# Retention and two feed-forward layers on one core: six weight slices converted beside the retention instead of nine, in halves, and PE filled while unit 1 loads

## The chip, the core and the metric

The kernel runs on one core of one Trainium2 chip. The metric is the device time of one execution in microseconds. Engines are named as in the profile: PE multiplies matrices (PEld is its weight load), DVE, ACT and POOL work element by element, and SP issues transfers; ACT and POOL issue some too.

## What is computed

Cut to what matters:

```python
# q, k, v: (4 batches, 8 heads, 768 positions, 64), float32
state = gamma[h] * state + outer(k[t], v[t])      # per batch and head, over t
y[t]  = q[t] @ state / 8
x = y as (3072 tokens, 512)
x = gelu_sigmoid(x @ w_in)  @ w_out               # 512 -> 2048 -> 512, first layer
x = relu(x @ w2_in) ** 2    @ w2_out              # 512 -> 2048 -> 512, second layer
```

## The kernel before, in words

**Retention.** The 3072 positions are cut into 24 units of 128 positions (six to a batch, all eight heads together). A unit is a block of 128 x 2048 floats (1.05 MB), loaded by SP in two halves of 0.52 MB: first q and k transposed for the scores, then k and v by position. There are five unit buffers, so SP issues unit u + 4 when the outputs of unit u - 1 have been computed. Iteration u of the loop at L564 puts in the queues: the scores of unit u on PE (L456) and its scaled values `vs` (on POOL for u < 6 and every third unit, L475, else eight small products on ACT, L480); for u = 2 to 5 the split of a unit of the first token block into a high and a low part (`split_0`, ACT L491 and DVE L492); the outputs of unit u - 1 on PE (L508, L519, L530); and then, within `cv_step`, the mask of unit u on DVE (L465) and the scaling of the outputs of unit u - 1 (L543, L547, L550). The scores have one buffer in PSUM: the scores of unit u + 1 wait for the mask of unit u.

**Weights of the first layer.** They come as 64-bit floats in 32 slices of 0.52 MB (16 steps f, each with one slice for up and one for down) and are converted on the chip: a load by POOL (`cv_load`, L119), two scalings on ACT (`cv_a`, L124 and L125), three operations on DVE (`join` in two steps, L129 and L134, `round_up`, L142), then a high part on ACT (`cv_high`, L157) and a low part on DVE (`cv_low`, L162). `cv_step` does one slice; in the retention it is given the mask and the scaling, which it queues between its own DVE operations. In the units of `CVU` a slice is converted, nine in all. `cv_step` there starts with `cv_a`, and loads begin at unit 2. The other 23 slices are converted in token block 0 of the first layer, seven in every four f.

**First layer.** Four blocks of 512 tokens (n = 0 to 3). For every f, `up(n, f)` gives PE 12 matmuls of 512 columns (L595 to L597), then ACT makes g and its high part gh (L602, L603) and DVE the low part gl (L607). `down(n, f - 2)` follows on PE with 12 more (L626 to L628); every third of them reads gl. After `up(3, 15)` come `down` of f = 13, 14 and 15 in a row, and then the second layer.

**Background.** The weights of a faster scheme for the rest of the work are made beside the layer by the generator `maker`. `background(us)` (L378) adds a credit and takes steps from `maker` until the credit is used up; each step states its own price in its `yield`. ACT's part of a step is put in `acts` and is queued only at the next call of `background`. Where `maker` needs such a part, it yields None, the call ends and the credit left over is capped at 3.0. `make_first` has 16 jobs, `make_second` 32 (lines 301 to 356). One call is made after every f but the last, as soon as the conversions are done. Each call gives `BG` = 4.8, but `BG - 1.6` = 3.2 for f >= 5 of block 3. In these f a step of `x_operands` (DVE, 128 x 1024) is queued as well: it prepares the next blocks, whose data `x_loads` fetches with POOL at f = 3.

Of the kernel before, what the change touches and what calls it, by code (L numbers as in the profile page):

```python
# [10 lines left out]
F32 = mybir.dt.float32  # L11
F32R = mybir.dt.float32r
BF16 = mybir.dt.bfloat16
U32 = mybir.dt.uint32
U16 = mybir.dt.uint16
ACTF = mybir.ActivationFunctionType
ALU = mybir.AluOpType
PSUM = bass.MemoryType.PSUM

P = 128  # L20
B, H, S, D = 4, 8, 768, 64
NT, DM, DFF = 3072, 512, 2048
NP = H // 2
CPB = S // P
NU = B * CPB
KD = DM // P
# [4 lines left out]
WA = 8  # L31
LOOK = 2
WARM = 10
UNITS = 5
# [6 lines left out]
NSTD = 4  # L41
SLOTS = 8
EARLY = 2
BG = 4.8
CVU = (5, 8, 11, 14, 17, 20, 21, 22, 23)
RAWS = 5
BGUP = 1.8

# [9 lines left out]
def tile_retention_then_two_ffns(  # L58
# [10 lines left out]
    nc = tc.nc  # L69
# [16 lines left out]
    cv_p = cv_ctx.enter_context(tc.tile_pool(name="cv", bufs=2, side="right"))  # L86
# [10 lines left out]
    order = []  # L97
# [5 lines left out]
            order.append((f, 1))  # L103
    wpool = {f: wa_p for f in range(WA)}
    ws = {}
    cv = {"load": 0, "a": 0, "b": 0, "pool": None, "ahead": 3}
    cvt = {}

    def cv_load():
        n = cv["load"]  # L110
        if n == len(order):
            return
        if n >= cv["b"] + cv["ahead"]:
            return
        cv["load"] += 1
        f, s = order[n]
        raw = cv_p.tile([P, 512, 2], U32, tag="raw", name=f"raw{n}", bufs=RAWS)
        src = w1[f, :, s * 512:(s + 1) * 512].bitcast(U32)
        nc.gpsimd.dma_start(out=raw, in_=src.rearrange("p (c t) -> p c t", t=2))  # L119
        cvt[n] = raw  # L120

    def scale_words(hm, raw):

        nc.scalar.mul(hm, raw[:, :, 1].bitcast(F32), 2.0 ** -112)  # L124
        nc.scalar.mul(raw[:, :, 0], raw[:, :, 0], 2.0 ** -29)  # L125

    def join(out, hb):

        v.tensor_scalar(  # L129
            out=out, in0=hb, scalar1=3, scalar2=0x7FFFFFFF,  # L130
            op0=ALU.logical_shift_left, op1=ALU.bitwise_and,
        )
        yield
        v.scalar_tensor_tensor(  # L134
            out=out, in0=hb, scalar=0x80000000, in1=out, op0=ALU.bitwise_and, op1=ALU.bitwise_or
        )
        yield

    def round_up(w, raw):

        half = w.bitcast(U16).rearrange("p (c t) -> p c t", t=2)[:, :, 0]
        v.scalar_tensor_tensor(out=half, in0=half, scalar=65527.0, in1=raw[:, :, 0], op0=ALU.min, op1=ALU.add)  # L142

    def cv_a():

        n = cv["a"]
        if n == min(cv["load"], cv["b"] + 2):
            return
        cv["a"] += 1
        scale_words(cvt[n][:, :, 1].bitcast(F32), cvt[n])  # L150

    held = deque()

    def cv_high():
        if held:
            w, hm, key = held[0]
            nc.scalar.copy(out=w[:, :, 0], in_=hm.rearrange("p (k c) -> p k c", c=P))  # L157

    def cv_low():
        if held:  # L160
            w, hm, key = held.popleft()
            v.tensor_tensor(  # L162
                out=w[:, :, 1], in0=hm.rearrange("p (k c) -> p k c", c=P), in1=w[:, :, 0], op=ALU.subtract
            )
            ws[key] = w

    def cv_step(limit=len(order), f1=None, f2=None, load=True):

        n, ready = cv["b"], cv["a"]
        if cv["pool"] is not None and limit is not None:  # L170
            cv_a()
        cv_high()
        if limit is None or n >= min(limit, ready):
            for f in (f1, f2):
                if f is not None:
                    f()
            cv_low()
        else:
            cv["b"] += 1
            raw = cvt.pop(n)  # L180
            key = order[n]
            hm = cv_p.tile([P, 512], F32, tag="hm", name=f"hm{n}")
            w = wpool[key[0]].tile([P, 4, 2, P], F32R, tag=f"w{key[1]}", name=f"w{n}")
            steps = join(hm.bitcast(U32), raw[:, :, 1])
            next(steps)
            if f1 is not None:
                f1()
            next(steps)
            round_up(hm, raw)
            if f2 is not None:  # L190
                f2()
            cv_low()
            held.append((w, hm, key))
        if limit is None:
            return
        if cv["pool"] is None:
            cv_a()
        if load:
            cv_load()
            cv_load()  # L200

    def weights(f, s):
        while (f, s) not in ws:
            if held:
                cv_high()
                cv_low()
            else:
                cv_step()
        return ws[f, s][:, :, 0], ws[f, s][:, :, 1]
# [168 lines left out]
    def background(us):  # L378

        credit[0] += us  # L380
        while acts:
            acts.popleft()()
        while credit[0] > 0:
            c = next(maker, None)
            if c is None:
                credit[0] = min(credit[0], 3.0)
                return
            credit[0] -= c
# [5 lines left out]
    hl = {}  # L394
# [15 lines left out]
    with tc.manual_schedule():  # L410

        with (
# [10 lines left out]
            warm_sb = att.tile([P, 512], BF16, tag="warm", name="warm_sb", bufs=1)  # L423
# [17 lines left out]
            def load_unit(u, parts=(0, 1024, 2048)):  # L441
                if u >= NU:
                    return
                if u not in units:
                    units[u] = att.tile([P, 2048], F32, tag="unit", name=f"unit{u}", bufs=UNITS)
                for a, z in zip(parts, parts[1:]):
                    nc.sync.dma_start(out=units[u][:, a:z], in_=qkv[u, :, a:z])
# [36 lines left out]
            def split_0():  # L484

                xt, cols = pend.pop("x", (None, None))
                if xt is None:
                    return
                for k in range(KD):
                    hi, lo = hl[0][k]  # L490
                    nc.scalar.copy(out=hi[:, cols], in_=xt[:, k, :])  # L491
                    nc.vector.tensor_tensor(  # L492
                        out=lo[:, cols], in0=xt[:, k, :], in1=hi[:, cols], op=ALU.subtract
                    )

            def banked(t):
                return t.rearrange("p (k b) i -> p b k i", b=2)
# [54 lines left out]

                return scaled

            load_unit(0, (0, 512, 1024))
            nc.sync.dma_start(out=tab_sb, in_=tab)
            load_unit(1, (0, 1024))
            load_unit(0, (1024, 2048))
            load_unit(1, (1024, 2048))
            nc.sync.dma_start(out=ytab_sb[0], in_=ytab)  # L560
            for u in range(2, UNITS):
                load_unit(u)

            for u in range(NU + 1):  # L564
                masked = scores(u) if u < NU else None
                split_0()
                scaled = outputs(u - 1) if u > 0 else None
                if 0 < u < CPB:
                    for p in range(NP):
                        nc.scalar.mul(ytab_sb[u][:, p, :], ytab_sb[0][:, p, :], ystep_sb[:, u, p:p + 1])  # L570
                if u == 18:
                    cv["ahead"] = RAWS
                cv_step(2 * WA if u in CVU else 0, masked, scaled, u >= 2)
                if u > 0:
                    load_unit(u + UNITS - 1)

# [13 lines left out]
        def up(n, f):  # L590
            hi, lo = weights(f, 0)
            hp = hp_p.tile([P, TB], F32, tag="h", name=f"h{n}_{f}")
            for k in range(KD):
                xh, xl = hl[n][k]
                nc.tensor.matmul(hp, lo[:, k], xh, start=(k == 0), stop=False)  # L595
                nc.tensor.matmul(hp, hi[:, k], xh, start=False, stop=False)  # L596
                nc.tensor.matmul(hp, hi[:, k], xl, start=False, stop=(k == KD - 1))  # L597
            g = g_p.tile([P, TB], F32, tag="gs", name=f"gs{n}_{f}", bufs=1)
            gh = g_p.tile([P, TB], F32R, tag="gh", name=f"gh{n}_{f}")
            gl = g_p.tile([P, TB], F32R, tag="gl", name=f"gl{n}_{f}")  # L600

            nc.scalar.activation(out=g, in_=hp, func=ACTF.Gelu_apprx_sigmoid)  # L602
            nc.scalar.copy(out=gh, in_=g)  # L603
            gs[n, f] = (gh, gl)

            def low():
                v.tensor_tensor(out=gl, in0=g, in1=gh, op=ALU.subtract)  # L607

            if n == 0 and cv["b"] < len(order):
                cv_step(len(order), None, low)  # L610
                if f % 4 < 3:
                    cv_step()
            else:
                low()
                if f < NF - 1:

                    background(BG if n < NSTD - 1 or f < 5 else BG - 1.6)

        def down(n, f):
            hi, lo = weights(f, 1)  # L620
# [233 lines left out]
        ready = deque()  # L854
# [212 lines left out]
```

## Time and profile before

| | us |
|---|---|
| median of 3 runs (1058.65 to 1060.0) | 1058.9 |
| profiled execution | 1059.31 |
| its span | 1057.5 |
| PE busy within the span | 1040.0 |
| DVE busy | 746.1 |
| ACT busy | 523.5 |

The span is the time from the first to the last instruction in the profile; 1.8 us lie around it. All times of rows are microseconds from the start of the span. "Busy" of PE counts matmuls whose ends are modelled, so it says where PE has work, not how fast it runs; the speed is seen from the distance between the starts of equal groups and from the granted clock.

### The profile page before, as it was taken

The numbers are of one execution on the slowest core, as the hardware profiler recorded it, in microseconds if no ns is written. First come the engines' busy times: TensorE is split into PE (matmuls) and PEld (weight loads), VectorE is DVE, ScalarE is ACT, GpSimd is POOL, SyncE is SP. The second block draws the span as 40 slices with busy tenths as digits, with TensorE's granted clock in tenths as the row PEclk, the third lists the DMA queues.
The fourth block names the chain that finished last, engine by engine and source line by source line (L and its number), as shares of the span: only waits on it lengthen the run. The fifth ranks groups of instructions, "written<-read, shape, count | busy, mean of one in ns | idle before, by whom it ended". The sixth has DMA issues, their size and how long they took to land.

```text
span 1057.5 us, 15484 instructions
## 1 busy us (share of the span) xinstructions
PE 1040.0 (98%) x5642; PEld 859.7 (81%) x5642; DVE 746.1 (71%) x1069; ACT 523.5 (49%) x858; POOL 101.5 (10%) x147
## 2 busy tenths in 40 slices
PE   7999999999999999999999999999999999999998
PEld 5887888888888888887888888888888888888886
DVE  3889997986787869753599344888345886455953
ACT  3768774434655667554546233455233464233443
POOL 2212210111111121110000100000100000000000
PEclk9999999999999999999999999999999999999999
DMA  9996879645588687799666876667876667766664
GB/s 342 366 405 219 329 257 357 248 189 191 201 262 268 236 306 255 261 349 321 191 214 217 269 236 193 192 208 225 302 197 192 188 216 232 218 193 188 209 205 161
DMA packets 106651, 259.34 MB, mean 245 GB/s; under 512 B 11216, under 2 KB 11344, under 8 KB 106320
## 3 DMA queue, kind: packets, MB, share of 16 engines
q1 hardware_dynamic: 79088, 156.64, 46.4%
q0 software_dynamic: 22304, 83.89, 22.5%
q10 hardware_dynamic: 5184, 17.83, 4.7%
q8 instruction: 45, 0.74, 0.3%
q14 instruction: 30, 0.25, 0.1%
HBM read 184.91 MB, written 73.40 MB: 244 GB/s over the span
## 4 chain that ended last, share of the span: by engine, by line
PE 92%; DMA 5%; DVE 1%; ACT 1%; SPq 0%; issue 0%; POOL 0%; ACTq 0%; POOLq 0%; DVEq 0%
PE D L769 29%; PE X L769 16%; PE Z L769 8%; PE h L595 6%; PE y L628 6%; PE y L626 5%; PE y L627 5%; PE h L596 5%; PE h L597 5%; PE Y L769 4%; DMA r<-kw 2%; DMA unit<-qkv 2%; PE yp L508 1%; PE sc L456 1%; DMA raw<-w 1%; DVE pt L465 1%
## 5 line engine op out<-in xcount | busy, mean ns | idle before, releaser
L769 PE MATMUL D<-gx,r 128*128 128x512 f32 x1344 | 306.4, 389 | 0.0
L769 PEld LDWEIGHTS D<-gx,r 128*128 128x128 f32 x1344 | 252.1, 188 | 53.0 <-DVE gx L872 0.8
L871 ACT CAST gx<-g 128x1024 fp32r<-128x1024 f32 x112 | 116.6, 1051 | 93.1 <-PE D L769 83.5
L872 DVE TENSOR_TENSOR gx<-g,gx 128x1024 fp32r<-128x1024 f32 x112 | 136.3, 1219 | 36.9 <-ACT gx L871 36.7
L769 PE MATMUL X<-xh,r 128*128 128x512 f32 x512 | 157.9, 390 | 1.1 <-DMA r<-kw 1.0
L790 ACT COPY g<-X 128x512 f32<-128x512 f32 x96 | 56.5, 589 | 188.9 <-PE X L769 188.9
L795 DVE TENSOR_TENSOR g<-Z,g 128x512 f32<-128x512 f32 x64 | 44.2, 691 | 147.5 <-ACT g L790 101.4
L769 PEld LDWEIGHTS X<-xh,r 128*128 128x128 f32 x512 | 95.8, 188 | 22.3 <-issue 2.7
L595 PE MATMUL h<-hl,w 128*128 128x512 f32 x256 | 99.7, 389 | 0.0
L628 PE MATMUL y<-gl,w 128*128 128x512 f32 x256 | 99.7, 389 | 0.0
L769 PE MATMUL X<-xl,r 128*128 128x512 f32 x256 | 99.6, 389 | 0.0
L627 PE MATMUL y<-gh,w 128*128 128x512 f32 x256 | 99.6, 389 | 0.0
L597 PE MATMUL h<-hl,w 128*128 128x512 f32 x256 | 99.6, 389 | 0.0
L626 PE MATMUL y<-gh,w 128*128 128x512 f32 x256 | 99.6, 389 | 0.0
L596 PE MATMUL h<-hl,w 128*128 128x512 f32 x256 | 99.6, 389 | 0.0
L769 PE MATMUL Z<-xh,r 128*128 128x512 f32 x256 | 79.0, 390 | 0.7 <-DMA r<-kw 0.7
L603 ACT CAST gh<-gs 128x512 fp32r<-128x512 f32 x64 | 39.8, 622 | 72.3 <-PE y L627 71.6
L607 DVE TENSOR_TENSOR gl<-gs,gh 128x512 fp32r<-128x512 f32 x64 | 44.1, 689 | 36.6 <-ACT gh L603 36.4
L602 ACT ACTIVATE gs<-h 128x512 f32<-128x512 f32 x64 | 38.1, 595 | 48.4 <-PE h L597 39.1
L769 PEld LDWEIGHTS Z<-xh,r 128*128 128x128 f32 x256 | 47.9, 188 | 11.2 <-issue 1.1
L628 PEld LDWEIGHTS y<-gl,w 128*128 128x128 f32 x256 | 48.1, 188 | 10.4 <-DVE gl L607 0.4
L595 PEld LDWEIGHTS h<-hl,w 128*128 128x128 f32 x256 | 48.1, 188 | 10.1 <-issue 0.2
(95 smaller groups left out, 1540.4 us busy)
## 6 DMA issues: line engine op xcount, KB each, us to landing
r<-kw SPq DMA_DIRECT2D x448, 256.0 KB, 2.9
kw<-wq POOLq DMA_DIRECT2D x32, 896.0 KB, 5.8
unit<-qkv SPq DMA_DIRECT2D x47, 512.0 KB, 8.9
raw<-w POOLq DMA_DIRECT2D x32, 512.0 KB, 6.7
kw<-wh POOLq DMA_DIRECT2D x16, 1024.0 KB, 4.7
kw<-w SPq DMA_DIRECT2D x16, 512.0 KB, 7.0
raw<-win ACTq DMA_DIRECT2D x16, 512.0 KB, 5.5
raw<-wout ACTq DMA_DIRECT2D x16, 512.0 KB, 4.1
```

The source lines that it names most:

```text
L595: nc.tensor.matmul(hp, lo[:, k], xh, start=(k == 0), stop=False)
L596: nc.tensor.matmul(hp, hi[:, k], xh, start=False, stop=False)
L597: nc.tensor.matmul(hp, hi[:, k], xl, start=False, stop=(k == KD - 1))
L607: v.tensor_tensor(out=gl, in0=g, in1=gh, op=ALU.subtract)
L626: nc.tensor.matmul(a, lo[:, e], gh, start=s0, stop=False)
L627: nc.tensor.matmul(a, hi[:, e], gh, start=False, stop=False)
L628: nc.tensor.matmul(a, hi[:, e], gl, start=False, stop=s1)
L769: nc.tensor.matmul(a, w, b, start=start, stop=stop, skip_group_check=True)
L790: nc.scalar.copy(out=t, in_=a)
L795: v.tensor_tensor(out=t, in0=a, in1=t, op=ALU.add)
L871: nc.scalar.copy(out=hi, in_=src)
L872: v.tensor_tensor(out=lo, in0=src, in1=hi, op=ALU.subtract)
```

## The change

The nine units of `CVU` go. From unit 12 on (`CV0`), a slice is converted over two units by the generator `convert`: its first join in one unit, its second join and rounding in the next, both queued on DVE behind the mask of the unit (`cv_unit`). The high part of a finished slice is the first thing on ACT in the next unit, and the low part on DVE comes behind that unit's mask. This gives six slices. Loads begin at unit 7 (`RAWU`), at most one per unit, and a slice is scaled on ACT at the end of a unit at least four units after its load was put in the queue (`cv_ahead`). The subtraction of `split_0` is queued behind the mask instead of ahead of it. The first loads of SP are reordered: unit 0's second half is ahead of unit 1's first, and unit 0's first half is one transfer. Eight matmuls on zeros follow the scores of unit 0 (`FILL`). In the first layer 26 slices are left to block 0, and the credit for f >= 5 of block 3 is `BG - 0.8` = 4.0.

```diff
-CVU = (5, 8, 11, 14, 17, 20, 21, 22, 23)
+CV0 = 12
+RAWU = 7
+FILL = 8
...
+    def convert():
+
+        n = cv["b"]
+        cv["b"] += 1
+        raw = cvt.pop(n)
+        key = order[n]
+        hm = cv_p.tile([P, 512], F32, tag="hm", name=f"hm{n}")
+        w = wpool[key[0]].tile([P, 4, 2, P], F32R, tag=f"w{key[1]}", name=f"w{n}")
+        steps = join(hm.bitcast(U32), raw[:, :, 1])
+        next(steps)
+        yield
+        next(steps)
+        round_up(hm, raw)
+        held.append((w, hm, key))
+
+    half = []
+
+    def cv_unit(u):
+
+        cv["step"] += 1
+        if half:
+            next(half.pop(), None)
+        else:
+            cv_low()
+            if CV0 <= u < NU and cv["b"] < cv["a"]:
+                half.append(convert())
+                next(half[0])
+
+    def cv_ahead(u):
+
+        if u == 18:
+            cv["ahead"] = RAWS
+        if u >= RAWU:
+            cv_load()
+        n = cv["a"]
+        if n < min(cv["load"], cv["b"] + 2) and cv["step"] >= loaded[n] + 4:
             cv_a()
+
+    def cv_step(f=None):
+
         cv_high()
-        if limit is None or n >= min(limit, ready):
...
+        old = bool(held)
+        if cv["b"] < cv["a"]:
+            for _ in convert():
+                pass
+        if f is not None:
+            f()
+        if old:
             cv_low()
...
-            load_unit(0, (0, 512, 1024))
+            load_unit(0, (0, 1024))
             nc.sync.dma_start(out=tab_sb, in_=tab)
-            load_unit(1, (0, 1024))
             load_unit(0, (1024, 2048))
-            load_unit(1, (1024, 2048))
+            load_unit(1)
+            load_unit(2, (0, 1024))
             nc.sync.dma_start(out=ytab_sb[0], in_=ytab)
-            for u in range(2, UNITS):
+            load_unit(2, (1024, 2048))
+            for u in range(3, UNITS):
                 load_unit(u)
 
             for u in range(NU + 1):
+                cv_high()
                 masked = scores(u) if u < NU else None
-                split_0()
+                if u == 0:
+                    fill = aps.tile([P, 2, NP, P], F32, tag="yp", name="fill")
+                    for i in range(FILL):
+                        nc.tensor.matmul(fill[:, 0, :, :], warm_sb[:, 0:P], warm_sb, start=True, stop=True)
+                low = split_0()
                 scaled = outputs(u - 1) if u > 0 else None
...
-                if u == 18:
-                    cv["ahead"] = RAWS
-                cv_step(2 * WA if u in CVU else 0, masked, scaled, u >= 2)
+                if masked is not None:
+                    masked()
+                if low is not None:
+                    low()
+                cv_unit(u)
+                if scaled is not None:
+                    scaled()
+                cv_ahead(u)
                 if u > 0:
                     load_unit(u + UNITS - 1)
...
             if n == 0 and cv["b"] < len(order):
-                cv_step(len(order), None, low)
+                cv_step(low)
                 if f % 4 < 3:
                     cv_step()
             else:
                 low()
                 if f < NF - 1:
 
-                    background(BG if n < NSTD - 1 or f < 5 else BG - 1.6)
+                    background(BG if n < NSTD - 1 or f < 5 else BG - 0.8)
```

## Rows read from the trace of the kernel before

**Rows 1.** Chain that ended last, from the page: shares of the span by engine

```profile
PE 92%; DMA 5%; DVE 1%; ACT 1%; SPq 0%; issue 0%; POOL 0%; ACTq 0%; POOLq 0%; DVEq 0%
```

**Rows 2.** Windows, first layer: busy PE, PEld, DVE, ACT, POOL; clock; DMA share; GB/s

```profile
91.00:178.00 87.00, 87.00 (x395) 71.90 (x388) 79.81 (x133) 59.60 (x106) 12.53 (x22) 1.00 0.80 283
...
420.00:440.00 20.00, 20.00 (x88) 16.25 (x87) 19.43 (x34) 10.55 (x16) 3.16 (x4) 1.00 0.65 220
```

**Rows 3.** Waits of PE before 230 us: total, times, longest

```profile
PE sc L456 <- DVE pt L465: 3.9, 4, 2.7
```

**Rows 4.** Timeline, units 0 to 2; start, duration, what, [idle before, releaser]

```profile
11.99 1.98 PE L508 MATMUL yp<-pt,vs 128*64 128x128 f32 x16 [1.59 <-POOL vs L475]
...
14.75 1.19 PE L456 MATMUL sc<-unit 64*128 64x128 f32 x16
```

**Rows 5.** Timeline, unit 5

```profile
24.30 0.68 ACT L124 ACTIVATE raw<-raw 128x512 f32<-128x512 f32 x1 [1.28 <-DMA raw<-w]
...
25.74 0.89 DVE L492 TENSOR_TENSOR hl<-x,hl 128x128 fp32r<-128x128 f32 x4 [3.01 <-ACT hl L491]
...
27.82 1.50 PE L456 MATMUL sc<-unit 64*128 64x128 f32 x16 [2.68 <-DVE pt L465]
```

**Rows 6.** PE's timeline, scores of units 13, 14, 15, 23; first feed-forward matmul

```profile
53.81 1.16 PE L456 MATMUL sc<-unit 64*128 64x128 f32 x16
...
56.49 1.16 PE L456 MATMUL sc<-unit 64*128 64x128 f32 x16
...
59.67 1.16 PE L456 MATMUL sc<-unit 64*128 64x128 f32 x16
...
85.44 1.16 PE L456 MATMUL sc<-unit 64*128 64x128 f32 x16 [0.19 <-DMA unit<-qkv]
...
91.22 0.50 PE L595 MATMUL h<-hl,w 128*128 128x512 f32 x1
```

**Rows 7.** Windows of 5 us in the retention; columns as in rows 2

```profile
10.00:15.00 5.00, 3.41 (x44) 3.10 (x42) 1.92 (x2) 0.13 (x1) 2.08 (x2) 0.66 1.02 393
...
20.00:25.00 5.00, 5.00 (x112) 4.47 (x110) 2.35 (x5) 2.44 (x8) 1.03 (x1) 1.00 1.02 411
...
40.00:45.00 5.00, 5.00 (x112) 4.40 (x108) 4.08 (x8) 1.73 (x6) 1.58 (x2) 1.00 0.99 343
...
80.00:85.00 5.00, 4.27 (x101) 3.80 (x96) 4.92 (x7) 3.79 (x12) 1.50 (x2) 1.00 1.03 408
```

**Rows 8.** Tile raw: duration of one in ns, least/median/most

```profile
L129 DVE TENSOR_SCALAR hm<-raw x32: 415/427/430, 29.9 to 158.6; 128x512 uint32<-128x512 uint32 x32
...
L134 DVE SCALAR_TENSOR_TENSOR hm<-raw,hm x32: 677/692/829, 31.4 to 159.1; 128x512 uint32<-128x512 uint32 x32
...
L142 DVE SCALAR_TENSOR_TENSOR hm<-hm,raw x32: 748/766/775, 32.1 to 159.8; 128x512 uint16<-128x512 uint16 x32
```

**Rows 9.** Timeline of DVE, the low part of a slice

```profile
46.04 0.69 DVE L162 TENSOR_TENSOR w<-hm,w 128x512 fp32r<-128x512 f32 x1 [0.74 <-ACT w L157]
```

**Rows 10.** Timeline of POOL, first and eleventh issue of a weight slice (eleven)

```profile
16.38 1.24 POOL L119 DMA_DIRECT2D raw<-w  x2
...
78.97 0.73 POOL L119 DMA_DIRECT2D raw<-w  x1 [6.86 <-DVE hm L142]
```

**Rows 11.** DVE's timeline in block 3: gl of f 6, 8 and 15

```profile
392.00 0.69 DVE L607 TENSOR_TENSOR gl<-gs,gh 128x512 fp32r<-128x512 f32 x1 [4.05 <-ACT gh L603]
...
403.13 0.68 DVE L607 TENSOR_TENSOR gl<-gs,gh 128x512 fp32r<-128x512 f32 x1
...
436.66 0.69 DVE L607 TENSOR_TENSOR gl<-gs,gh 128x512 fp32r<-128x512 f32 x1
```

**Rows 12.** Timeline of ACT in block 3: the last x block

```profile
389.77 1.05 ACT L654 CAST xh<-xb 128x1024 fp32r<-128x1024 f32 x1 [3.61 <-DMA xb<-xkept]
```

**Rows 13.** PE's timeline: first matmul on gl(15), first of layer 2

```profile
437.40 0.50 PE L628 MATMUL y<-gl,w 128*128 128x512 f32 x1
...
439.81 0.62 PE L769 MATMUL X<-xh,r 128*128 128x512 f32 x2
```

More of the change, by code (lines that the diff above doesn't have):

```diff
@@ L105, in tile_retention_then_two_ffns @@
     ws = {}
-    cv = {"load": 0, "a": 0, "b": 0, "pool": None, "ahead": 3}
+    cv = {"load": 0, "a": 0, "b": 0, "pool": None, "ahead": 3, "step": 0}
+    loaded = {}
     cvt = {}
@@ L120, in cv_load @@
         cvt[n] = raw
+        loaded[n] = cv["step"]
     def scale_words(hm, raw):
@@ L165, in cv_low @@
             ws[key] = w
-    def cv_step(limit=len(order), f1=None, f2=None, load=True):
-        n, ready = cv["b"], cv["a"]
-        if cv["pool"] is not None and limit is not None:
+    def convert():
[28 more added lines that the diff above has]
+        if n < min(cv["load"], cv["b"] + 2) and cv["step"] >= loaded[n] + 4:
             cv_a()
+    def cv_step(f=None):
         cv_high()
-        if limit is None or n >= min(limit, ready):
-            for f in (f1, f2):
-                if f is not None:
-                    f()
-            cv_low()
[L178 to L200, printed above, removed]
+        old = bool(held)
[5 more added lines that the diff above has]
+        if old:
+            cv_low()
+        cv_a()
+        cv_load()
+        cv_load()
     def weights(f, s):
@@ L487, in split_0, with low @@
                 if xt is None:
-                    return
+                    return None
                 for k in range(KD):
[L490 to L494, printed above, removed]
+                    nc.scalar.copy(out=hl[0][k][0][:, cols], in_=xt[:, k, :])
+                def low():
+                    for k in range(KD):
+                        hi, lo = hl[0][k]
+                        nc.vector.tensor_tensor(
+                            out=lo[:, cols], in0=xt[:, k, :], in1=hi[:, cols], op=ALU.subtract
+                        )
+                return low
             def banked(t):
```

## Prediction

> **What bounds the kernel now.** I read the page's chain first: 92% of the span hangs on PE [rows 1]. So what counts is where PE waits or runs slowly. The windows show that the feed-forward part has no hole: PE is busy for 87 of 87 us in its first block [rows 2]. The list of PE's waits before 230 us puts the largest part in the retention: scores (L456) waiting 3.9 us for the masks of DVE [rows 3]. The timeline then gives the two soft places and their causes.
>
> The first is units 0 and 1. The outputs of unit 0 start only at 11.99, after 1.59 us of waiting for POOL, and their 16 matmuls take 1.98 us where unit 13's step from 56.49 to 59.67 holds the same 16 and three other groups in 3.18 [rows 4, 6]; the scores of unit 2 start at 14.75 [rows 4].
>
> The second is unit 5. ACT stands at 24.30 for a weight slice that has just landed (1.28 us idle, releaser the transfer). Behind it in ACT's queue lie the copies for the split of x; DVE's split (25.74, 3.01 us idle) waits for those, the mask waits behind the split, and PE's scores start 2.68 us late and cold: 1.50 us for 16 matmuls instead of 1.16 [rows 5, 6].
>
> A third bound is under both: the transfers. They move 411 GB/s at 20 to 25 us and 408 at 80 to 85, only 343 at 40 to 45 when PE's delays keep SP from issuing [rows 7]. The last unit's scores start when its transfer lands, 85.44, and the first feed-forward matmul is at 91.22, 5.78 us later [rows 6].
>
> **Part 1: the retention.** A unit costs PE 3.18 us (56.49 to 59.67), or about 2.7 at a batch's edge (53.81 to 56.49) [rows 6]. From the scores of unit 2 to those of unit 23 are 15 steps of 3.18 and 6 of 2.7: 63.9 us. Measured: 85.44 - 14.75 = 70.7 [rows 4, 6]. So 6.8 us are lost there, and that much could go if nothing else were late.
>
> Unit 5's stall goes: slices are loaded from unit 7 and scaled at least four units later, at the end of ACT's work for the unit, so ACT no longer stands on a weight transfer, and the split's subtraction is queued behind the mask. DVE per slice: 0.43 + 0.69 + 0.77 + 0.69 = 2.6 us [rows 8, 9]; in pairs of units it costs 1.3 a unit beside a mask and a scaling, about 1.9 together, so 3.2 against PE's 3.0 to 3.18. It nearly fits; the old form piled all 2.6 on one unit, and on each of the last four. The start: unit 0's second half now lands before unit 1's first half; the eight fill matmuls only use time in which PE waits. The scores of unit 2 start between 13.5 (outputs of unit 0 at full clock, about 1.2 us saved) and 14.75 (nothing saved). I take neither, because the end is set elsewhere.
>
> What is late next is the transfer queue. PE alone would bring unit 11's scores to 14.75 + 27.7 = 42.4 or a little before. From there twelve units of 1.05 MB and about seven slices of 0.52 MB must land: 16.3 MB, at 405 GB/s 40.2 us, less a lead of about 4 us that the buffers give: the last unit lands at 78 to 79. From the other side: before, eleven slices had been issued (16.38 to 78.97 [rows 10]) when it landed at 85.44. One or two fewer save 1.3 us each, and the thin stretch around 40 us (62 GB/s short, some 15 us: 0.9 MB) 2.3: 80.5 to 81.8. I take 80. Then the tail: 5.78 with today's crowding of DVE, 4.8 if PE alone sets it (a step of 3.18 for unit 23's scores and unit 22's outputs, and 2.7 - 1.1 for unit 23's outputs, an edge unit's step without its scores [rows 6]). I take 5.5: the first feed-forward matmul at 85.5, a gain of **5.7 us**, bounds 4 and 8.
>
> A rule of the Trainium skill speaks against even this: "DMA: Bandwidth & Descriptors", Specifications, gives a limit of about 358 GB/s from HBM for one core. The trace disagrees: 411 and 408 GB/s in two windows [rows 7], so the rows decide. By 358 the 16.3 MB would take 45.5 us instead of 40.2, and nearly all of the gain would go.
>
> **Part 2: three slices more in the feed-forward.** 26 instead of 23 slices are converted in block 0, seven per four f. Up(f) needs 2f slices; 6 + 1.75f are there, so the weights stay ahead (at f = 8: 20 for 17). DVE's extra 3 x 2.6 = 7.8 us in block 0 take the place of the two background calls at f = 13 and 14, which held about as much, and PE has no hole there to widen [rows 2]. Cost 0 while that holds; were it all exposed, 7.8.
>
> **Part 3: the background credit, 3.2 to 4.0 for f >= 5 of block 3.** This is the step that I price highest. A second-layer job asks 4.15 credits (0.45 + 0.7 + 0.7 + 1.1 + 0.6 + 0.6, lines 329 to 354) and can't run twice in one call, since the next job's scaling is only queued then. Leftover credit is capped at 3.0. Today ten calls have 3 + 32 = 35 credits: 8.4 jobs. After: 43, so every call runs a whole job.
>
> What a whole job costs in this stretch is seen at f = 6 and 7, where stored credit still pays for it: from the gl of f = 6 (392.00) to that of f = 8 (403.13) are 11.13 us, 5.57 per f, for one gl, one job and one step of the x operands [rows 11]. PE needs 24 matmuls per f; 1536 lie between 91.22 and 439.81 [rows 6, 13], 0.227 each, 5.45 us. So DVE is slower than PE for as long as full jobs run. DVE is full already (19.43 of 20 us at 420 to 440 [rows 2]). Today the smaller credit lets it catch up: the gl of f = 15 starts at 436.66 instead of 392.00 + 9 x 5.57 = 442.1 [rows 11]. And it is needed at once: PE's first matmul on it starts at 437.40, just after it, 0.14 behind its beat [rows 13]. With 5.4 us more queued ahead of it, gl of f = 15 ends at 442.7, and PE, which can't go on to the last accumulations without it, waits **5.3 us** more, in two pieces: about 2.6 on f = 14 and 2.7 on f = 15.
>
> The lower bound: DVE's lag begins with 4.05 us of idling at f = 6, because ACT's queue stood for the last x block, cast at 389.77 after 3.61 us [rows 11, 12]. If that block lands early, the whole queue moves up by as much: 1.3 us. The upper bound is 5.3.
>
> What follows such waits: after 1.59 us of idling unit 0's outputs took from 11.99 to 14.75, 2.76 us, for work of about 1.5 [rows 4], and the granted clock of that stretch is 0.66 [rows 7], part of it at the lower of its two levels (1.2 of 2.4 GHz); after 2.68 us the same shows [rows 5]. I take 1.2 us for that, bounds 0 and 2.5 (both waits paid).
>
> **The sum.** Profiled execution 1059.31 (span 1057.5 and 1.8 around it) - 5.7 + 5.3 + 1.2 = 1060.1. The median of the runs lies 0.4 lower: **1059.7**. The gain of the first 90 us is given back at 440.
>
> **Rivals.**
> - Forecast, stall eats gain: 1057 to 1062. 0.52.
> - *The stall is hidden.* The last x block lands early enough, or DVE's queue holds less than I count; only 1.3 us are lost: 1059.3 - 5.7 + 1.3 - 0.4 = 1054.5. For: 4.05 us of DVE idling are there to be used. Against: the loads are issued at the same f with the same traffic. 0.22.
> - *Slower: the clock.* It falls in the first of the two waits at the end of block 3, and the retention gains only 4: 1059.3 - 4 + 5.3 + 2.5 - 0.4 = 1062.7. It decides once PE stands for 2.6 us, as at unit 5 [rows 5]. 0.15.
> - *Slower: the queues don't deliver.* With slices bunched behind POOL's work for units 12, 18 and 21, transfers go at 343 as at 40 to 45 [rows 7]: 47.5 us for the 16.3 MB, 7.3 more: 1059.3 + 1.6 + 5.3 + 1.2 - 0.4 = 1067. The figure of the Trainium skill above is this case in a milder form. 0.08.
> - *Weights run dry in block 0*, 7.8 more: 1067. 0.03.
>
> **How the numbers follow.** What a measurement of this kernel tells from no change is about 0.2%, 2.1 us: faster is below 1056.8, slower above 1061.0. Faster: 0.20 of the second case and 0.05 of the forecast's lower edge, 0.25. Slower: 0.14 of the clock, 0.08, 0.03 and 0.08 of the forecast's upper edge, 0.33. Same: 0.42. The ends of the costs are -8 + 1.3 and -4 + 5.3 + 2.5, so 1052.2 to 1062.7; leaving out the farthest of both, 1053.5 to 1063.0 holds about 0.85.
>
> **What would show it.** Right: the first feed-forward matmul at 84 to 87; no wait of ACT's scaling for a weight transfer before unit 12; PE's scores of units 21 to 23 waiting for their transfers; in block 3 gl 5.57 us apart from f = 6 on, and PE waiting for gl of f = 14 and 15 with over 4 us in total, then some us at a lower granted clock. Wrong: PE without a hole between the retention and the second layer (then the time is near 1054), or the first feed-forward matmul at 90 or later (then over 1063).

## The result, and the profile after

The changed kernel takes 1065.1 us (median of 6 runs, 1063.3 to 1066.3) against 1058.7 before: a ratio of 1.0059, 95% interval 1.0046 to 1.0072. It is slower by 6 us, where 1059.7 and a range up to 1063.0 had been predicted. The profiled execution took 1066.25, the longest of the six, with a span of 1064.5, 7.0 more than the span before.

Three points cut the span into parts: the first feed-forward matmul, the first of the second layer, and the end. PE's timeline of the changed kernel gives them (start, duration, what, and in brackets the idle time before and its releaser); the first four rows are the scores of units 2, 20, 22 and 23.

```profile
11.88 1.16 PE L478 MATMUL sc<-unit 64*128 64x128 f32 x16
...
67.49 1.16 PE L478 MATMUL sc<-unit 64*128 64x128 f32 x16
...
75.99 1.56 PE L478 MATMUL sc<-unit 64*128 64x128 f32 x16 [1.92 <-DVE xout L574]
...
80.76 1.16 PE L478 MATMUL sc<-unit 64*128 64x128 f32 x16
...
85.56 0.50 PE L633 MATMUL h<-hl,w 128*128 128x512 f32 x1
...
431.03 0.50 PE L666 MATMUL y<-gl,w 128*128 128x512 f32 x1 [2.01 <-DVE gl L645]
...
436.59 0.50 PE L666 MATMUL y<-gl,w 128*128 128x512 f32 x1 [0.95 <-DVE gl L645]
...
439.00 0.61 PE L807 MATMUL X<-xh,r 128*128 128x512 f32 x2
...
459.56 1.22 PE L807 MATMUL X<-xh,r 128*128 128x512 f32 x2 [4.51 <-ACT g L828]
```

Against rows 6 and 13 this gives

| part | before | after | difference |
|---|---|---|---|
| start to first feed-forward matmul | 91.22 | 85.56 | -5.7 |
| first layer | 348.59 | 353.44 | +4.85 |
| second layer | 617.69 | 625.5 | +7.8 |

The first two were forecast (-5.7, and +5.3 with 1.2 for the clock). The third was not in the prediction at all. "First layer" stands here for its four blocks n = 0 to 3 alone, and "second layer", here as in the prediction, for all that comes after them: by the list `blocks` in the kernel, that begins with the first layer's last two token blocks, done by the faster scheme.

**The first layer's loss.** DVE's timeline in block 3, gl of f = 6, 7, 14 and 15, which answers to rows 11:

```profile
385.85 0.69 DVE L645 TENSOR_TENSOR gl<-gs,gh 128x512 fp32r<-128x512 f32 x1 [4.55 <-ACT gh L641]
391.41 0.68 DVE L645 TENSOR_TENSOR gl<-gs,gh 128x512 fp32r<-128x512 f32 x1
...
430.30 0.68 DVE L645 TENSOR_TENSOR gl<-gs,gh 128x512 fp32r<-128x512 f32 x1
435.85 0.69 DVE L645 TENSOR_TENSOR gl<-gs,gh 128x512 fp32r<-128x512 f32 x1
```

Nine steps in 50.0 us, 5.56 each, against PE's 5.45: every call now runs a whole job. PE's waits at 431.03 and 436.59 end just after gl of f = 14 and f = 15.

**The second layer's loss.** ACT's timeline shows what PE's wait at 459.56 hangs on. ACTq is the issue of a transfer by ACT.

```profile
440.57 0.34 ACTq L269 DMA_DIRECT2D raw<-wout  x1
...
449.36 0.66 ACT L128 ACTIVATE hm<-raw 128x512 f32<-128x512 f32 x1 [2.51 <-DMA raw<-wout]
449.37 0.33 ACTq L269 DMA_DIRECT2D raw<-wout  x1
...
457.83 0.67 ACT L128 ACTIVATE hm<-raw 128x512 f32<-128x512 f32 x1 [4.92 <-DMA raw<-wout]
...
458.95 0.56 ACT L828 COPY g<-X 128x512 f32<-128x512 f32 x1
```

A slice issued at 449.37 lands 8.5 us later. ACT comes to it at the next background call, at 452.91, only 3.5 us after the issue. It stands for 4.92 us, and behind it in its queue lies the copy of X that PE needs. The issue itself was late because ACT had stood for 2.51 us before it: the load lies behind the scaling of the slice issued at 440.57. The windows of these stretches (us, length, busy PE, PEld, DVE, ACT, POOL, clock, DMA share, GB/s) show the price:

```profile
430.00:435.00 5.00, 3.97 (x10) 3.13 (x11) 4.84 (x11) 1.43 (x3) 0.72 (x1) 0.66 0.56 199
455.00:460.00 5.00, 0.49 (x2) 0.44 (x2) 0.00 (x0) 2.17 (x5) 0.40 (x1) 0.89 1.05 401
460.00:465.00 5.00, 5.00 (x13) 3.89 (x13) 1.82 (x6) 1.15 (x3) 0.00 (x0) 0.50 0.54 177
465.00:470.00 5.00, 5.00 (x22) 4.06 (x21) 1.83 (x4) 3.69 (x6) 0.00 (x0) 0.93 0.74 223
```

The transfer engines are full (share 1.05) while ACT stands. After the wait PE runs at 0.50 of its clock for these 5 us, that is at the lower level: 13 matmuls where the kernel before has 24 in the same window. So by an estimate from these rows, 4.5 us of waiting cost about 2.5 more in the window that follows and 0.35 in the next (0.93). With the 0.4 us by which PE's waits for its weights r grow (2.4 against 2.0), that is the 7.8.

### The profile page after: what moved, and what is told of

It is laid out like the page before. It is cut to its first block, busy times and chain, and to the rows that moved or that the text cites. A ratio compares the mean times of both kernels' runs of the same rounds, so it can differ in the third digit from the quotient of the medians.

```text
span 1064.5 us, 15503 instructions
## 1 busy us (share of the span) xinstructions
PE 1044.9 (98%) x5650; PEld 862.4 (81%) x5650; DVE 748.1 (70%) x1069; ACT 524.2 (49%) x858; POOL 100.9 (9%) x147
## 4 chain that ended last, share of the span: by engine, by line
PE 90%; DMA 5%; DVE 3%; issue 1%; ACT 0%; SPq 0%; DVEq 0%
PE D L807 29%; PE X L807 16%; PE Z L807 8%; PE h L633 5%; PE h L634 5%; PE h L635 5%; PE y L666 5%; PE y L665 5%; PE y L664 5%; PE Y L807 4%; DMA unit<-qkv 2%; PE sc L478 2%; PE yp L535 2%; DMA raw<-wout 2%; DMA r<-kw 1%; PE yp L557 1%
## 5 line engine op out<-in xcount | busy, mean ns | idle before, releaser
L807 PE MATMUL X<-xh,r 128*128 128x512 f32 x512 | 160.3, 395 | 6.1 <-ACT g L828 4.5
L807 PEld LDWEIGHTS X<-xl,r 128*128 128x128 f32 x256 | 48.8, 191 | 10.3
```

What stands on the lines that cost most here:

```text
L807: nc.tensor.matmul(a, w, b, start=start, stop=stop, skip_group_check=True)
```

## The experiments

Two theories stood at the start. **A**: all of the loss is the credit's, at both places. **B**: only the wait on gl is; the second layer loses because things arrive there earlier and with two background calls fewer. C is a rival on the transfer, D to G are about single parts. Line numbers shift by a few between kernels; names don't.

**e1: the credit put back.**

```diff
-                    background(BG if n < NSTD - 1 or f < 5 else BG - 0.8)
+                    background(BG if n < NSTD - 1 or f < 5 else BG - 1.6)
```

> The changed kernel with the credit of block 3 put back to 3.2 per call; all else as changed. Theory A (the credit makes all of the loss, twice: 4.9 us because gl of f = 15 comes late, and 7.8 us in the first products of the second layer, where ACT stands for a weight transfer because the credit left over brings two jobs in two calls): the retention's 5.7 us remain, 1053.0 (1052 to 1054.5), no PE wait on gl above 0.3 us, no PE wait on ACT near the start of the second layer. Theory B (only the 4.9 us are the credit's; the second layer loses its 7.8 us because everything arrives there 5 us earlier and with two background calls fewer): 1060 to 1061, the wait on ACT still there.

Measured 1054.85 us, ratio 0.9962 (0.9949 to 0.9975). PE's timeline, first matmuls of the two layers:

```profile
85.71 0.50 PE L633 MATMUL h<-hl,w 128*128 128x512 f32 x1
...
434.07 0.61 PE L807 MATMUL X<-xh,r 128*128 128x512 f32 x2
```

The first layer is back at 348.36 us without any wait on gl, though block 0 still converts 26 slices. The second layer takes 619.0, 6.5 less than in the changed kernel; a wait of 1.1 us on ACT is left, of the same kind. The time is 0.35 above the upper end of A's range, and A had left no wait on ACT; B's 1060 is out.

**e2: the credit alone, on the kernel before.** The same line there, `BG - 1.6` to `BG - 0.8`.

> The kernel before with one edit, the credit of block 3 raised from 3.2 to 4.0. Theory A: 1058.7 + 4.9 + 7.8 = 1071 (1069 to 1073), both waits as in the changed kernel. Theory B: 1058.7 + 4.9 = 1063.6, only the wait on gl.

Measured 1063.5 us, 1.0041 (1.0025 to 1.0056): B's number, and a miss for A. The first layer takes 352.83 us (+4.2), the second 617.65, as before. The waits on gl are 1.36 and 2.52 us, and the granted clock stays at 1.00 behind both (435 to 450 us). ACT's timeline shows why the second layer loses nothing. These are all its loads of slices from 440 us on, and of each scaling the first instruction:

```profile
446.53 0.34 ACTq L247 DMA_DIRECT2D raw<-wout  x1
447.00 0.66 ACT L124 ACTIVATE hm<-raw 128x512 f32<-128x512 f32 x1
455.41 0.66 ACT L124 ACTIVATE hm<-raw 128x512 f32<-128x512 f32 x1 [2.59 <-DMA raw<-wout]
```

With two background calls more in block 0, fewer jobs are left: the load that hurt the changed kernel is the one after these, and here there is none. So the second loss needs both the credit and the jobs that the deferred conversions leave over.

**e3: the phase alone.** The changed kernel with

```diff
         first_ctx.close()
+        credit[0] = -0.05
```

> The changed kernel, but the credit left over at the end of block 3 is set to -0.05, as in the kernel before, instead of 1.5. Theory A: the wait on gl stays (4.9 us), the one on ACT in the second layer goes with its cold clock: 1058.5 (1057 to 1060). Theory B: 1065, unchanged.

Measured 1059.14 us, 1.0002 (0.9992 to 1.0013), as A has it. ACT's loads and scalings between 448 and 458 us, of each scaling the first instruction:

```profile
448.75 0.68 ACT L128 ACTIVATE hm<-raw 128x512 f32<-128x512 f32 x1 [0.54 <-DMA raw<-wout]
448.76 0.33 ACTq L269 DMA_DIRECT2D raw<-wout  x1
...
457.15 0.35 ACTq L269 DMA_DIRECT2D raw<-wout  x1
457.63 0.67 ACT L128 ACTIVATE hm<-raw 128x512 f32<-128x512 f32 x1
```

The slice issued at 448.76 is scaled at 457.63, 8.9 us after its issue, and no wait stands in that row: with the other credit ACT comes to it one call later, when it has landed. The second layer takes 616.74 us. The wait on gl is still there, 4.9 us in this profile:

```profile
431.07 0.50 PE L666 MATMUL y<-gl,w 128*128 128x512 f32 x1 [2.31 <-DVE gl L645]
...
436.62 0.50 PE L666 MATMUL y<-gl,w 128*128 128x512 f32 x1 [2.54 <-DVE gl L645]
...
440.46 0.77 PE L808 MATMUL X<-xh,r 128*128 128x512 f32 x2
```

Up to the end of block 3 this is the code of the changed kernel, yet the first layer takes 355.20 us here, 6.6 more than before and 1.8 more than in the changed kernel's profile. The granted clock stays at 1.00 behind the first wait (430 to 435 us) and is 0.50 behind the second (437.5 to 440 us).

**e5: the loads issued by POOL.** The changed kernel with

```diff
-                later(lambda n=n: load(n + 2))
+                load(n + 2)
...
-            nc.scalar.dma_start(out=raws[n], in_=src...
+            (nc.scalar if n < 2 else nc.gpsimd).dma_start(out=raws[n], in_=src...
```

> The changed kernel, but the loads of the second layer's weight slices are issued by POOL as soon as the buffer is free, a background call earlier than by ACT. Theory A (ACT's scaling stands for a load that was issued one call before it): the waits of ACT for these loads go, and with them PE's wait on ACT: 1058.5 (1057 to 1060). Rival C (the transfer engines are full at 450 to 460 us, so the slice lands no earlier whoever issues it): 1065 and the same wait of ACT.

Measured 1057.2 us, 0.9980 (0.9967 to 0.9993), at the lower end of A's range. ACT's waits between 380 and 500 us (total, times, longest), first of the changed kernel, then of e5:

```profile
ACT hm L128 <- DMA raw<-wout: 8.6, 3, 4.9
```

```profile
ACT hm L128 <- DMA raw<-wout: 0.9, 2, 0.5
```

The waits go, and PE's wait on ACT with them. Rival C falls: the transfers are still slow in this stretch (the loads issued at 443.10 and 450.82 take 6.5 and 6.4 us to land), but issued earlier they have landed, or nearly so, when ACT comes to them. The edit changes the engine and the moment of the issue together; the two weren't tried apart. The time is lower by 8 us with the credit still at 4.0, and not all of that is the second layer's: it takes 617.05 us in this profile, 8.45 less than in the changed kernel, and the first layer 351.34, 2.1 less, since DVE stands for 2.50 us before gl of f = 6 where it stood for 4.55.

**e10 and e11: credit 3.2 and loads by POOL**, two runs of the same kernel (e1's and e5's edits).

> As e1, and the loads of the second layer's weight slices issued by POOL as in e5. Theory A: PE's wait of 1.1 us on ACT in the second layer goes too: 1053.0 to 1054.0. Rival C: 1054.9.

> The kernel of e10 once more (retention as changed, credit 3.2, slices of the second layer loaded by POOL), to stand beside e12 to e14 on one chip. All theories: a ratio of 0.992 to 0.995 to the kernel before, 1051 to 1053.5 where before is 1058.8; first feed-forward matmul at 85.3 to 87.3.

Measured 1052.0 us, 0.9925 (0.9906 to 0.9944), and 1050.15, 0.9908 (0.9895 to 0.9922): both below the ranges that were expected, so theory A leaves out a part of the gain. Windows of the second layer's crowded stretch, of the kernel before, the changed one, e1 and e11 in turn:

```profile
440.00:520.00 80.00, 77.97 (x339) 62.87 (x338) 36.58 (x61) 40.81 (x68) 7.63 (x11) 1.00 0.88 302
```

```profile
440.00:520.00 80.00, 73.10 (x304) 58.32 (x303) 35.01 (x59) 37.87 (x64) 7.41 (x10) 0.96 0.86 292
```

```profile
440.00:520.00 80.00, 76.36 (x332) 61.68 (x331) 42.63 (x72) 42.84 (x72) 7.79 (x10) 1.00 0.94 329
```

```profile
440.00:520.00 80.00, 79.84 (x353) 65.74 (x352) 47.46 (x76) 45.00 (x74) 9.53 (x13) 1.00 0.92 329
```

PE is busy for 79.84 of 80 us in e11: its waits for r are gone too (0.2 us). Why the loads by POOL take those with them wasn't tried on its own and stays open.

**e14: the loads by POOL on the kernel before.**

> The kernel before with one edit, the slices of the second layer loaded by POOL. Theory A (only a phase that brings ACT to the slice too early pays, and the kernel before has none in the second layer): 1058.0 to 1059.0. Theory G (the earlier loads also take transfers out of the crowded stretch at 450 to 500 us, where PE waits for its weights r 1.0 + 0.7 + 0.3 us): 1056 to 1057.

Measured 1057.75 us, 0.9982 (0.9973 to 0.9991). The time lies between A's range and G's; the gain, 1.8 us on the 1059.54 which the kernel before took beside it, lies at the small end of G's. PE still waits 1.6 us for r there, 2.0 before, and the second layer takes 616.6 us, 1.1 less than before. So most of what the edit gives e11 over e1, 4.7 us of second layer (614.3 against 619.0), is not there on the kernel before. It may hang on the jobs left over; that wasn't tried.

**e9: nine slices, spread.** On e1:

```diff
-CV0 = 12
-RAWU = 7
+CV0 = 6
+RAWU = 1
```

> As e1, but nine slices as before the change, each spread over two units, from unit 6 on with loads from unit 1 on. Theory A: three slices more before the last unit, 3.9 us: first feed-forward matmul at 89 to 90, time 1058 to 1059; so the number of slices makes most of the 5.7 us, not the spreading. Rival F (the gain is that ACT no longer stands on slices and that DVE's work is spread; the number matters little): first feed-forward matmul at 85.7 to 87, time 1054.9 to 1056.

Measured 1057.66 us, 0.9980 (0.9969 to 0.9990), first feed-forward matmul at

```profile
89.19 0.50 PE L633 MATMUL h<-hl,w 128*128 128x512 f32 x1
```

as A has it: 3.5 us for three slices. The time is 0.3 us below A's range. PE waits 6.1 us for transfers of units in it, 2.8 in e1.

**e7: two loads fewer.** On e1, `cv["ahead"]` stays 3 in the whole retention.

> As e1, but loads of slices never run more than three ahead in the retention, so two slices fewer are moved before the last unit lands. Theory A (transfer floor, 0.52 MB at 405 GB/s is 1.3 us a slice): first feed-forward matmul at 83.0 to 84.0 instead of 85.7, time 1052.5 to 1053.5 unless block 0's scaling then stands for slices that are still to come. Rival E (the end is set by DVE and POOL work of units 21 to 23): first feed-forward matmul at 85.7, time 1054.9.

Measured 1055.0 us, 0.9953 (0.9937 to 0.9970), first feed-forward matmul at 85.21. A's 83 to 84 is missed. The retention of e1, e3, e5, e10, e11 and the changed kernel is the same code and ends between 85.26 and 87.28, so 85.21 tells little; POOL's queue shows that only one load moved behind the last unit. Inconclusive.

**e13: three slices.** On e11, `CV0 = 18`, `RAWU = 13`.

> As e11, with three slices in the retention (from unit 18, loads from unit 13) instead of six. Theory A: with three slices fewer on the way PE alone sets the retention, first feed-forward matmul at 82 to 83.5; 29 slices are then left for block 0, where up of f = 13 and later waits for weights, so the time is 1052 to 1058. Theory E (POOL's and DVE's work in the last units sets the end): 85 to 87.

The first feed-forward matmul comes at 83.06, as A has it. But the time is 1124.9 us, 1.0614 (1.0599 to 1.0628), 67 above the upper expectation. PE's longest wait in its list (total, times, longest), and one window of block 0:

```profile
PE h L633 <- DVE w L166: 40.4, 12, 4.5
```

```profile
140.00:160.00 20.00, 13.15 (x44) 9.89 (x42) 7.69 (x14) 7.87 (x15) 1.66 (x3) 0.84 0.44 145
```

Once `up` waits for its own slice, no engine is full (DVE 7.7 and ACT 7.9 of 20 us), and the granted clock is lower (0.84). My reading, not tried on its own, is that slice, g and matmuls follow one another in a ring through in-order queues. I had priced running dry by DVE's work, 2.6 us a slice; that is far too low.

**e6 and e12: the old start**, old load order and `FILL = 0`, once on e1 and once on e11.

> As e1 (credit 3.2), but with the first loads in the old order and no fill matmuls. Theory A (the retention's end is set by the transfers, so units 0 to 2 may be late at no cost): scores of unit 2 at about 14.7 instead of 11.9, first feed-forward matmul at 85.2 to 86.2 as in e1 (85.71), time 1054.9 within 1. Rival D (PE's order sets the end, the start counts in full): first feed-forward matmul at 88.5, time 1057.7.

> As e11, with the first loads in the old order and no fill matmuls. Theory A (the transfers set the retention's end, the start costs nothing): same as e11 within 1 us. Theory D (the 2.9 us by which the scores of unit 2 come later are paid at least by half): 1.4 to 3 us above e11; e6 gave a first feed-forward matmul at 88.77, which speaks for D, and a ratio as e1, which speaks for A.

e6 gave 1056.0 us and 0.9964 (0.9951 to 0.9977), no different from e1's ratio, measured on another chip. Its first feed-forward matmul comes at 88.77, 3.1 us later than e1's, as D has it, and its second layer is 1.3 us shorter (617.7), so its time decides nothing. e12, on one chip with e11, gave 1053.6, 0.9944 (0.9932 to 0.9957): 3.5 us slower than e11, with intervals apart. Scores of units 2, 3 and 20 and the first feed-forward matmul, e11 and then e12:

```profile
12.20 1.16 PE L478 MATMUL sc<-unit 64*128 64x128 f32 x16
...
15.59 1.16 PE L478 MATMUL sc<-unit 64*128 64x128 f32 x16
...
67.76 1.16 PE L478 MATMUL sc<-unit 64*128 64x128 f32 x16
...
85.51 0.50 PE L633 MATMUL h<-hl,w 128*128 128x512 f32 x1
```

```profile
13.60 2.08 PE L478 MATMUL sc<-unit 64*128 64x128 f32 x16 [0.41 <-DMA unit<-qkv]
...
19.42 1.25 PE L478 MATMUL sc<-unit 64*128 64x128 f32 x16
...
71.48 1.16 PE L478 MATMUL sc<-unit 64*128 64x128 f32 x16
...
89.46 0.50 PE L632 MATMUL h<-hl,w 128*128 128x512 f32 x1
```

At unit 3 e12 is 3.8 us late, at unit 20 3.7, and from there to the first feed-forward matmul both take nearly the same, 17.75 and 17.98 us. What is lost at the start is paid in full: theory D, and by more than it said (1.4 to 3 us). Unit 2's scores run slowly in e12 (2.08 us for 16 matmuls, granted clock 0.54 from 15 to 20 us), at full speed in e11, after the fill. Load order and fill were put back together, so their shares are not known.

## Why the prediction was wrong, point by point

**The step that failed: the second layer was put at nothing, without a reason.** The sum had the term "1.2 for the clock" behind the waits of block 3 and nothing after it; the profile showed 7.8 us lost there, by the wait of ACT for a slice issued one background call before (4.92 us), PE's wait behind it (4.51) and the lower clock after that. No row of the kernel before from behind block 3 was read for it. Yet the same working gives what was needed: ten jobs out of 43 credits leave 1.5 over, where the kernel before ends at about zero, and two background calls fewer leave more jobs to do. I used the credit only for how many jobs run, not for where the queue stands when the second layer begins. e3 shows that the phase alone moves 6 us, e2 that it needs the jobs left over, e5 that an earlier issue of the loads takes the wait away.

**Part 3 was right**: 5.56 us per f (forecast 5.57), whole jobs in all calls, PE waiting on gl of f = 14 and 15. e2 shows the same kind of loss, 4.2 us, on the kernel before with this edit alone, and e1 that it goes when the credit is put back. The size, 5.3 + 1.2, was too large against the 4.85 of the changed kernel's profile: there PE runs at the lower level between the two waits (clock 0.66), which stretches its ten matmuls there by an estimated 1.7 us (0.34 of 5), but this time is part of the wait for gl of f = 15, and the waits shown are only 3.0 in sum. Added, both were counted twice. In e3, with the same code, the lower level came behind the second wait, and the loss was 6.6, as the sum had it. So the sum held for one of two executions, and it gave no way to tell which.

**Part 1 has the right sum from a wrong step, and in part by luck.** The end of 85.5 and the gain of 5.7 were met (85.56, 5.7), but two errors cancel in it: the last unit's scores came at 80.76 where 80 was taken, and the tail took 4.80 where 5.5 was. The wait of PE before unit 22 (1.92 us at 75.99) is, by the profile's releaser, one for DVE; but by the trace the first half of unit 22, issued at 65.08, lands at 75.86, and in e1, e3, e5, e9, e11 and e13, too, these scores start 0.13 or 0.14 us after that landing. So it is most likely the wait for a transfer that was forecast for units 21 to 23. Behind it the step to unit 23 takes 4.77 us, with a granted clock of 0.66 from 75 to 80 us.

"I take neither, because the end is set elsewhere" is the step of part 1 that failed: unit 2's scores came at 11.88, earlier than both values, and the start was worth about 3.5 us (e12 against e11). I had treated the transfers as a fixed floor; they follow PE, since SP issues a unit's load when PE frees its buffer (it stands 32.0 us for PE's outputs in the changed kernel), and the wait of the last units is added to whatever came before. That slices cost transfer time held: 3.5 us for three more (e9), 2.2 to 4.2 for three fewer (e13), against 3.9 worked out. Start and slices together come to more than the 5.7, so they can't simply be added, and what the spreading over two units is worth alone wasn't tried. The figure of the Trainium skill ("DMA: Bandwidth & Descriptors", Specifications) that was weighed against this part was rightly set aside: the changed kernel moves 407 and 408 GB/s from 20 to 60 us.

**Part 2 was right**: e1's first layer takes 348.36 us with 26 slices in block 0. The rival "weights run dry" didn't occur, but 7.8 priced DVE's work alone: e13, which does run dry with 29 slices in block 0, is over 70 us slower than e11.

**The rivals.** "The stall is hidden" didn't come: the last x block was no earlier (DVE idles 4.55 us there, before 4.05). "Slower: the clock" had the right sign and a part of the cause, at the wrong place: the lower clock cost most in the second layer, after a wait of 4.5 us that no case named. The range's upper end, 1063.0, is above the 1062.7 to which the prediction's own costs come, so "leaving out the farthest" narrowed the lower side alone.

## What to carry to other kernels

When a credit or a priority of background work is changed, follow not only how much work it queues but where its queue stands at the start of the next stage, and which loads are then one call old. A load that an engine issues shortly before it consumes the data itself can stop everything else in that engine's queue; issued by POOL as soon as the buffer is free, the same loads left ACT waiting for 0.9 us instead of 8.6. A wait and the slow clock after it must not be added where the slow work runs inside the next wait, and must be where it doesn't; one profile doesn't tell which will happen in the next execution.

## What the runs showed of the hardware that was not expected

A slice of 0.52 MB took 8.5 us to land when the transfer engines were at a share of 1.0 and 400 GB/s; the median of the changed kernel's loads of such slices from 380 to 470 us is 4.2 us. And a wait of PE for 2.0 us in the middle of dense work was followed by a granted clock of 0.66 over the 5 us around it; after 4.5 us it was 0.50 for 5 us and 0.93 for the next. Yet in e3, with the same code up to there, a wait of 2.31 us was followed by 1.00 and one of 2.54 us by 0.50, and in e2 one of 2.52 us by 1.00. So in these runs the length of a wait alone does not tell whether the clock falls.
